# A float64 weight conversion that works in the tile it fills, on one Trainium2 core

## The chip, the core and the metric

The kernel runs on one core of a Trainium2 chip. Five engines work side by side: TensorE (PE; its weight loads are PEld), VectorE (DVE), ScalarE (ACT), GpSimd (POOL) and SyncE (SP, which here issues the loads). Each runs its own queue of instructions in order, and they wait for one another by semaphores. The metric is the device time of one execution in microseconds (us).

## The reference

Three layers follow one another. The attention inputs are float32; the two weights of the second layer (`moe_w_in`, `moe_w_out`) are scaled by a double and reach the chip as float64.

```python
out_up, out_local = ...                      # attention over means of 4, and over a band of 7 positions
x = (out_up + out_local)                     # 4 batches, 8 heads, 576 positions, 64 wide -> 2304 x 512
h = x @ w_in                                 # 512 x 2048, float64 weights
g = np.maximum(h, 0.0) + np.log1p(np.exp(-np.abs(h)))
y = (g @ w_out).astype(np.float32)           # 2048 x 512, float64 weights
logits = y @ w_gate + modality_bias[modality_id]
e_idx = np.argmax(logits, axis=1)            # one expert of 8 for each row
out[mask] = gate_w[mask, None] * (np.maximum(y[mask] @ w1[e], 0.0) @ w2[e])
```

## The kernel before

The 2304 rows go through the second layer in six blocks `n` of 384. A block has sixteen chunks `c` of 128 hidden columns: `mlp_H(n, c)` makes the product with `w_in` in a PSUM tile `ph` and starts softplus on ACT (three instructions on the tile `ga`, lines 777 to 779); `mlp_g` finishes it on VectorE (`gN` at line 786 for the first eight chunks of block 0, line 793 elsewhere); `mlp_Y` (line 802), three chunks later, adds the product with `w_out` to four PSUM tiles `py`. Block 0 uses plain float32 (lines 768 and 809); later blocks and the second half of block 0's `mlp_Y` use weights split in two float32r parts (`wis`, `wos`, lines 667 and 668).

Attention of batch 0 runs ahead of block 0, that of batches 1 to 3 is spread over the blocks. In one attention step `pS` holds scores, `ls` the masked scores, `lst` their maxima and sums, three ACT exponentials (line 341) fill `ls`, POOL scales it (line 347), PE transposes it to `pA`, VectorE copies that to `laT` (line 355), and PE makes `pO` of it.

The weights are converted while this goes on, in the first 157 us, and only there. There are 32 tiles of 128 by 512: sixteen of `w_in` into the tile `wi`, sixteen of `w_out` into `wo`. For each, SP loads the raw 8-byte words into a tile `raw` (512 KB; lines 642 and 646); ACT takes the absolute value of the upper halves, scaled, as float32 (`f64_top`, line 617), and three VectorE instructions turn the bits into a float32 number (`from_f64`, lines 625, 628 and 629). The first two of them work in a small tile `cva`, of which there are two, and the third writes to `wi` or `wo`. `raw` has six buffers, which it shares with the attention loads `qr`, `kr` and `vr`, so a load of a tile waits until a buffer is free, and a `raw` is free when its three readers are done.

The order of instructions on each engine is set by a scheduler when the kernel is built: it runs an own timeline of the program and takes what its timeline calls ready, with the priority that `ahead` asks for. `from_f64`'s first instruction is held in program order. What is ready for the scheduler depends on the buffers, so a change in buffers can change the order too.

Of the kernel before, what the change touches and what calls it, by code (L numbers as in the profile page):

```python
# [9 lines left out]
F32 = mybir.dt.float32  # L10
F32R = mybir.dt.float32r
I32 = mybir.dt.int32
U32 = mybir.dt.uint32
AF = mybir.ActivationFunctionType
ALU = mybir.AluOpType
# [26 lines left out]
F64_REBIAS = 2.0 ** -112  # L42
# [15 lines left out]
def band_attention__softplus_mlp__top1_moe(  # L58
# [15 lines left out]
    V, A, G, T = nc.vector, nc.scalar, nc.gpsimd, nc.tensor  # L74
# [28 lines left out]
    mlp = ctx.enter_context(tc.tile_pool(name="mlp", bufs=2))  # L103
    wi = wpool.tile([128, NC1, CC, 128], F32, name="wi")
    wo = wpool.tile([128, NC1, DM], F32, name="wo")
    ydram = drp.tile([NB, 128, CC, TB], F32, name="ydram")

    def ahead(n):

        return tc.high_priority(n) if n else nullcontext()  # L110
# [478 lines left out]
    for n in range(NOLD):  # L589
        for st in range(6):  # L590
            if (n, st) not in done:
                late = n >= 14
                t = {3: 8.0, 4: 8.6 if late else 8.0, 5: 9.0 if late else 8.3}[st]
# [18 lines left out]
                    )  # L612


    def f64_top(raw):
        t = mlp.tile([128, 512], I32, tag="cva", name="cva", bufs=2)
        A.activation(t.bitcast(F32), raw[:, :, 1].bitcast(F32), AF.Abs, scale=F64_REBIAS)
        return t

    def from_f64(raw, t, dst):  # L620

        lo, hi = raw[:, :, 0], raw[:, :, 1]
        ins = V.tensor_scalar(t, t, 3, None, ALU.logical_shift_left)  # L625
        if started[0]:
            tc.keep_in_program_order(ins)
        V.scalar_tensor_tensor(t, hi, -0x80000000, t, ALU.bitwise_and, ALU.bitwise_or)  # L628
        V.scalar_tensor_tensor(dst.bitcast(I32), lo, 29, t, ALU.logical_shift_right, ALU.bitwise_or)  # L629

    conv = [("i", 0), ("i", 1), ("o", 0)]
    for c in range(1, NC1):
        conv += ([("i", c + 1)] if c + 1 < NC1 else []) + [("o", c)]
    cpos, lpos = [0], [0]
    raws, tops = {}, {}

    def load_raw(n):
        while lpos[0] < min(n, len(conv)):
            kind, c = conv[lpos[0]]
            raw = mlp.tile([128, 512, 2], I32, tag="raw", name="raw", bufs=RAWB)  # L640
            if kind == "i":
                nc.sync.dma_start(
                    out=raw.rearrange("p (c f) w -> p c (f w)", c=CC),
                    in_=w_in[:, c * 128:(c + 1) * 128].bitcast(I32).rearrange("(c p) f -> p c f", p=128))
            else:
                nc.sync.dma_start(out=raw.rearrange("p f w -> p (f w)"),
                                  in_=w_out[c * 128:(c + 1) * 128, :].bitcast(I32))
            raws[lpos[0]] = raw
            lpos[0] += 1

    def conv_to(n):
        while cpos[0] < min(n, len(conv)):
            i = cpos[0]
            load_raw(i + 2)
            kind, c = conv[i]
            with ahead(0 if started[0] else -50):
                for k in range(i, min(i + 2, lpos[0]) if started[0] else i + 1):
                    if k not in tops:
                        tops[k] = f64_top(raws[k])
                from_f64(raws.pop(i), tops.pop(i), wi[:, c].rearrange("p c f -> p (c f)") if kind == "i" else wo[:, c, :])  # L660
            cpos[0] += 1
            load_raw(i + 2)

# [359 lines left out]
    for st in range(HEAD):  # L1023
        attn_to(pre_end[st])
        if st >= C0 - 5 + LAG:
            conv_to((st - C0 + 5 - LAG) * CR // 4 + 1)
        if st == 9 + LAG:
            split_wi(0, 0)
# [16 lines left out]
    for i, (n, c) in enumerate(seq[:NMLP]):  # L1045
# [20 lines left out]
        if n == 0:  # L1066
            conv_to(max(cpos[0], 3 + 2 * c + 1, CB + (33 - CB) * (2 * c + 1) // 32))
# [21 lines left out]
        if n == 0:  # L1089
            conv_to(max(cpos[0], 3 + 2 * c + 2, CB + (33 - CB) * (2 * c + 2) // 32))  # L1090
# [97 lines left out]
    p, q, pos_q = stages[-1]  # L1188
# [57 lines left out]
```

## Time and profile before

| | |
|---|---|
| time, median of 3 runs | 764.23 us (763.49 to 765.17) |
| the profiled execution | 765.59 us, of which the span of its instructions is 763.8 us |
| mean granted TensorE clock | 0.991 of full speed |
| TensorE matmul busy | 734.5 us, 96% of the span |
| VectorE busy | 487.6 us, 64% |
| ScalarE busy | 462.3 us, 61% |
| GpSimd busy | 419.2 us, 55% |

All times in rows are us from the start of the span. A busy PE is not a PE at its peak, since matmuls overlap in its pipe and their ends are modelled. An idle time with a name behind it is the time that the engine stood before this instruction, and what let it go.

### The profile page before, as it was taken

The page shows a single profiled execution, that of the slowest core. Times are in us where ns is not written, and L with a number is a line of the kernel's source. Part 1 is how long each engine was busy: PE and PEld are TensorE (multiplying, and loading weights), DVE is VectorE, ACT ScalarE, POOL GpSimd, SP SyncE. Part 2 cuts the span into 40 slices and gives each one's busy share as a digit, 9 for nine tenths or more (in the row PEclk, how much of TensorE's full clock was granted, in tenths as well). Part 3 has the DMA queues.
Part 4 walks back from the last instruction along what each step waited for, and adds up shares of the span by engine and source line. Part 5 has one row for each costly group of instructions (what it writes and reads, how often), then busy time and mean ns, then how long its engine had stood idle before and what let it go on. Part 6 is the DMA issues. An engine that isn't in the chain of part 4 may idle for free.

```text
span 763.8 us, 13608 instructions
## 1 busy us (share of the span) xinstructions
PE 734.5 (96%) x4917; PEld 655.8 (86%) x4918; DVE 487.6 (64%) x933; ACT 462.3 (61%) x1196; POOL 419.2 (55%) x381
## 2 busy tenths in 40 slices
PE   5989899999999999999999999999999999999995
PEld 5765567699999999998999999999997989899894
DVE  6999779765879555788645554346994484284222
ACT  5955565676667757666766665666864364365332
POOL 3553207376565655665565656666778465455542
PEclk9989999999999999999999999999999999999999
DMA  8987755115230511241001100530011022002002
GB/s 190 203 188 195 226 165 177 45 39 106 50 75 9 112 33 23 42 87 42 14 2 23 43 1 1 221 125 1 4 68 55 21 63 83 0 1 83 1 0 88
DMA packets 111446, 55.45 MB, mean 73 GB/s; under 512 B 89593, under 2 KB 102411, under 8 KB 111371
## 3 DMA queue, kind: packets, MB, share of 16 engines
q1 hardware_dynamic: 111083, 53.98, 26.8%
q8 instruction: 41, 0.67, 0.4%
q10 hardware_dynamic: 288, 0.52, 0.2%
q14 instruction: 34, 0.28, 0.1%
HBM read 45.05 MB, written 9.44 MB: 71 GB/s over the span
## 4 chain that ended last, share of the span: by engine, by line
PE 69%; DVE 16%; ACT 4%; issue 4%; DMA 3%; POOL 2%; SPq 1%; DVEq 0%; ACTq 0%; POOLq 0%
PE ph L771 19%; PE py L812 19%; PE py L1130 11%; PE ph L973 9%; PE pS L462 2%; DVE cva L628 2%; PE pO L495 2%; DVE cva L625 2%; PE pA L488 1%; PE py L809 1%; DVE xs L954 1%; DMA vr<-in_v_dram 1%; DVE wi L629 1%; DMA raw<-in_moe_w_in_dram 1%; PE ph L768 1%
## 5 line engine op out<-in xcount | busy, mean ns | idle before, releaser
L812 PE MATMUL py<-g,wos 128*128 128x384 f32 x1056 | 209.1, 341 | 2.6 <-DVE y L818 1.2
L812 PEld LDWEIGHTS py<-g,wos 128*128 128x128 f32 x1056 | 182.6, 188 | 9.2 <-issue 1.4
L771 PE MATMUL ph<-xT,wis 128*128 128x384 f32 x960 | 182.2, 337 | 0.0
L771 PEld LDWEIGHTS ph<-xT,wis 128*128 128x128 f32 x960 | 166.7, 188 | 1.1
L668 POOL TENSOR_TENSOR wis<-wi,wis 128x512 fp32r<-128x512 f32 x80 | 104.1, 1304 | 73.0 <-ACT wis L667 66.2
L668 POOL TENSOR_TENSOR wos<-wo,wos 128x512 fp32r<-128x512 f32 x88 | 118.2, 1344 | 45.0 <-ACT wos L667 44.7
L777 ACT ACTIVATE ga<-ph 128x384 f32<-128x384 f32 x96 | 46.6, 485 | 64.3 <-PE ph L771 61.3
L793 DVE SCALAR_TENSOR_TENSOR ph<-ph,ga 128x384 f32<-128x384 f32 x80 | 44.7, 560 | 58.9 <-ACT ga L779 58.6
L973 PE MATMUL ph<-xs,ws 128*128 128x384 f32 x378 | 73.9, 336 | 1.2 <-DVE u L978 1.2
L978 DVE TENSOR_TENSOR u<-ph,u 128x384 f32<-128x384 f32 x60 | 33.3, 555 | 60.2 <-PE ph L973 59.9
L973 PEld LDWEIGHTS ph<-xs,ws 128*128 128x128 f32 x378 | 67.1, 188 | 4.8 <-DVE u L978 1.6
L667 ACT CAST wos<-wo 128x512 fp32r<-128x512 f32 x88 | 54.4, 618 | 26.4 <-PE py L812 23.6
L1130 PE MATMUL py<-wos,gs 128*128 128x512 f32 x270 | 69.0, 394 | 0.7 <-POOL gs L984 0.4
L1130 PEld LDWEIGHTS py<-wos,gs 128*128 128x128 f32 x270 | 50.0, 188 | 9.8 <-POOL gs L984 0.8
L668 POOL TENSOR_TENSOR wos<-w2s,wos 128x512 fp32r<-128x512 f32 x24 | 33.5, 1395 | 34.7 <-ACT wos L667 34.7
L779 ACT ACTIVATE ga<-ga 128x384 f32<-128x384 f32 x96 | 50.3, 525 | 2.1
L778 ACT ACTIVATE ga<-ga 128x384 f32<-128x384 f32 x96 | 50.3, 525 | 0.3
L481 POOL TENSOR_TENSOR pls<-pls,plst 128x420 f32<-128x420 f32 x18 | 16.0, 891 | 61.2 <-DVE plst L480 54.4
L475 ACT ACTIVATE pls<-pls,plst 128x70 f32<-128x70 f32 x108 | 36.7, 341 | 21.4 <-DVE plst L473 21.3
L794 DVE CAST g<-ph 128x384 fp32r<-128x384 f32 x80 | 44.0, 550 | 7.8 <-PE py L812 4.3
L667 ACT CAST wis<-wi 128x512 fp32r<-128x512 f32 x80 | 48.9, 611 | 0.0
L768 PE MATMUL ph<-xN,wi 128*128 128x384 f32 x128 | 45.6, 503 | 0.9 <-DVE gN L786 0.9
(195 smaller groups left out, 1232.4 us busy)
## 6 DMA issues: line engine op xcount, KB each, us to landing
raw<-in_moe_w_in_dram SPq DMA_DIRECT2D x16, 512.0 KB
raw<-in_moe_w_out_dram SPq DMA_DIRECT2D x16, 512.0 KB
lv<-in_v_dram SPq DMA_DIRECT2D x72, 70.0 KB
vr<-in_v_dram SPq DMA_DIRECT2D x16, 288.0 KB
ydram<-y SPq DMA_DIRECT2D x12, 384.0 KB
yb<-ydram SPq DMA_DIRECT2D x12, 384.0 KB
out_dram<-ob SPq DMA_DIRECT2D x16, 256.0 KB
qr<-in_q_dram SPq DMA_DIRECT2D x48, 72.0 KB
```

The lines of the kernel that those rows point to most:

```text
L667: A.copy(w[:, 0], src)
L668: G.tensor_tensor(out=w[:, 1], in0=src, in1=w[:, 0].bitcast(F32), op=ALU.subtract)
L768: T.matmul(ps[:, :TB], wi[:, c, cc, :], xT[n][:, cc, :], start=(cc == 0), stop=(cc == CC - 1))
L771: T.matmul(ps[:, :TB], wt[:, w, cc, :], xT[n][:, x, cc, :], start=(i == 0), stop=(i == 3 * CC - 1))
L777: A.activation(a, ps[:, :TB], AF.Abs)
L778: A.activation(a, a, AF.Exp, scale=-1.0)
L779: A.activation(a, a, AF.Ln, bias=1.0)
L793: V.scalar_tensor_tensor(o, ps[:, :TB], 0.0, a, ALU.max, ALU.add)
L794: (A.copy if n < NATIVE else V.tensor_copy)(g[:, 0, :], o)
L812: T.matmul(yps[n][dc][:, :TB], w[:, a, dsl], g[:, b, :], start=(c == 0 and i == 0), stop=(c == NC1 - 1 and i == 2))
L973: T.matmul(ps[:, :TB], ops[:, w, a, cc, :], xop[p, x][:, l, cc, :], start=i == 0, stop=i == 5)
L1130: T.matmul(yps[n][t], g[:, a, t * 128:(t + 1) * 128], w[:, b, :], start=first and c == q and i == 0, stop=last and c == q + NQ and i == 2)
```

## The change

`cva` is gone. ACT writes the absolute value straight into the 128 by 512 part of `wi` or `wo` that the conversion fills, and the three VectorE instructions work there in place. Each part is written once in the program, so ACT no longer has a buffer to wait for. The number, the operations and the sizes of the instructions stay: 32 on ACT and 96 on VectorE. The two `cva` buffers stay allocated, as output tiles (`ob`) of the last stage use the same tag.

```diff
-    def f64_top(raw):
-        t = mlp.tile([128, 512], I32, tag="cva", name="cva", bufs=2)
-        A.activation(t.bitcast(F32), raw[:, :, 1].bitcast(F32), AF.Abs, scale=F64_REBIAS)
-        return t
-
-    def from_f64(raw, t, dst):
...
-        lo, hi = raw[:, :, 0], raw[:, :, 1]
+    def f64_top(raw, dst):
+        A.activation(dst, raw[:, :, 1].bitcast(F32), AF.Abs, scale=F64_REBIAS)
+
+    def from_f64(raw, dst):
...
+        lo, hi, t = raw[:, :, 0], raw[:, :, 1], dst.bitcast(I32)
         ins = V.tensor_scalar(t, t, 3, None, ALU.logical_shift_left)
...
-        V.scalar_tensor_tensor(dst.bitcast(I32), lo, 29, t, ALU.logical_shift_right, ALU.bitwise_or)
+        V.scalar_tensor_tensor(t, lo, 29, t, ALU.logical_shift_right, ALU.bitwise_or)
...
+    def weights(i):
+        kind, c = conv[i]
+        return wi[:, c].rearrange("p c f -> p (c f)") if kind == "i" else wo[:, c, :]
...
                 for k in range(i, min(i + 2, lpos[0]) if started[0] else i + 1):
-                    if k not in tops:
-                        tops[k] = f64_top(raws[k])
-                from_f64(raws.pop(i), tops.pop(i), wi[:, c].rearrange("p c f -> p (c f)") if kind == "i" else wo[:, c, :])
+                    if k not in topped:
+                        topped.add(k)
+                        f64_top(raws[k], weights(k))
+                from_f64(raws.pop(i), weights(i))
```

In the new file `f64_top` is line 616, `from_f64` lines 623, 626 and 627, and later lines are three higher (softplus is 780 to 782). The build puts instructions of block 0 in another order, on ACT most of all; behind block 0 the orders agree.

ACT before, from the exponentials of the last attention step but one of batch 0 (`ls_808`) to the end of the first softplus (`ga_887`; numbers behind a name tell one tile from the next, and the brackets hold the engines or load queues whose semaphores are awaited):

```order
L341 ACTIVATE ls_808,lst_810<-ls_808,lst_810 128x70 [waits DVE_49,PE_49,Pool_49]
L341 ACTIVATE ls_808,lst_810<-ls_808,lst_810 128x70 x2
L341 ACTIVATE ls_845,lst_847<-ls_845,lst_847 128x70 [waits DVE_49,PE_49,Pool_49]
L341 ACTIVATE ls_845,lst_847<-ls_845,lst_847 128x70 x2
L384 CAST xT_918<-xf_919 128x192 [waits DVE_49]
L777 ACTIVATE ga_887<-ph_882 128x384 [waits PE_49]
L778 ACTIVATE ga_887<-ga_887 128x384 [waits Activation_49]
L384 CAST xT_918<-xf_930 128x192 [waits DVE_49]
L779 ACTIVATE ga_887<-ga_887 128x384 [waits Activation_49]
```

The same place on ACT in the changed kernel (`ls_805` and `ls_842` are those two steps, `ga_883` the first softplus):

```order
L341 ACTIVATE ls_805,lst_807<-ls_805,lst_807 128x70 [waits DVE_49,PE_49,Pool_49]
L341 ACTIVATE ls_805,lst_807<-ls_805,lst_807 128x70 x2
L616 ACTIVATE wi_95<-raw_957 128x512 [waits DMAHW2_49]
L341 ACTIVATE ls_842,lst_844<-ls_842,lst_844 128x70 [waits DVE_49,PE_49,Pool_49]
L341 ACTIVATE ls_842,lst_844<-ls_842,lst_844 128x70 x2
L616 ACTIVATE wo_96<-raw_984 128x512 [waits DMAHW6_49]
L384 CAST xT_912<-xf_913 128x192 [waits DVE_49]
L780 ACTIVATE ga_883<-ph_878 128x384 [waits PE_49]
L616 ACTIVATE wi_95<-raw_998 128x512 [waits DMAHW7_49]
L781 ACTIVATE ga_883<-ga_883 128x384 [waits Activation_49]
L384 CAST xT_912<-xf_924 128x192 [waits DVE_49]
L782 ACTIVATE ga_883<-ga_883 128x384 [waits Activation_49]
```

Three first steps of conversions, the eighth to tenth of the 32, stand here now, and they wait for a load alone.

ACT before, at the softplus of chunk 3 (`ga_1076`), behind the exponentials of a pair of attention steps (`pde`):

```order
L416 ACTIVATE pde_1050,pdn_1049<-pS_1040,pmx_1048 96x144 x2
L617 ACTIVATE cva_1103<-raw_1101 128x512 [waits DMAHW6_49,DVE_49]
L777 ACTIVATE ga_1076<-ph_1071 128x384 [waits PE_49]
L778 ACTIVATE ga_1076<-ga_1076 128x384 [waits Activation_49]
L617 ACTIVATE cva_1122<-raw_1120 128x512 [waits DMAHW0_49,DVE_49]
L779 ACTIVATE ga_1076<-ga_1076 128x384 [waits Activation_49]
```

The same place on ACT in the changed kernel (the softplus of chunk 3 is `ga_1066`):

```order
L416 ACTIVATE pde_1040,pdn_1039<-pS_1030,pmx_1038 96x144 x2
L616 ACTIVATE wo_96<-raw_1108 128x512 [waits DMAHW1_49]
L616 ACTIVATE wi_95<-raw_1120 128x512 [waits DMAHW2_49]
L616 ACTIVATE wo_96<-raw_1135 128x512 [waits DMAHW3_49]
L780 ACTIVATE ga_1066<-ph_1061 128x384 [waits PE_49]
L781 ACTIVATE ga_1066<-ga_1066 128x384 [waits Activation_49]
L616 ACTIVATE wi_95<-raw_1147 128x512 [waits DMAHW4_49]
L782 ACTIVATE ga_1066<-ga_1066 128x384 [waits Activation_49]
```

Where two first steps stood around the softplus before, four stand now, three of them ahead of it and one inside.

## Rows read from the trace of the kernel before

**Rows 1.** The page: busy time, share of the span and instructions of each engine.

```profile
PE 734.5 (96%) x4917; PEld 655.8 (86%) x4918; DVE 487.6 (64%) x933; ACT 462.3 (61%) x1196; POOL 419.2 (55%) x381
```

**Rows 2.** Waits over the span: engine, tile, line, releaser: us, times, longest.

```profile
ACT cva L617 <- DVE wi L629: 12.7, 8, 2.3
...
ACT cva L617 <- DVE wo L629: 11.0, 10, 2.3
```

**Rows 3.** Waits of PE from 55 to 165 us.

```profile
PE pA L430 <- DVE gN L786: 2.1, 1, 2.1
...
PE py L812 <- POOL g L795: 0.9, 1, 0.9
...
PE ph L768 <- DVE gN L786: 0.9, 1, 0.9
...
PE pA L430 <- DVE ga L793: 0.7, 1, 0.7
...
PE pO L495 <- DVE plaT L489: 0.4, 1, 0.4
```

**Rows 4.** Tile `cva`: durations in ns (min/median/max), first and last start, forms.

```profile
L617 ACT ACTIVATE cva<-raw x32: 641/678/707, 27.9 to 149.4; 128x512 f32<-128x512 f32 x32
...
L628 DVE SCALAR_TENSOR_TENSOR cva<-raw,cva x32: 650/691/1652, 29.6 to 155.5; 128x512 int32<-128x512 int32 x32
L629 DVE SCALAR_TENSOR_TENSOR wi<-raw,cva x16: 650/691/2002, 31.1 to 148.5; 128x512 int32<-128x512 int32 x16
```

**Rows 5.** Timeline of ACT, 57 to 62 us: start, us, instruction, [idle before, releaser].

```profile
57.60 0.35 ACT L341 ACTIVATE ls<-ls,lst 128x70 f32<-128x70 f32 x1 [1.91 <-DVE lst L335]
...
60.48 0.49 ACT L777 ACTIVATE ga<-ph 128x384 f32<-128x384 f32 x1
61.00 0.52 ACT L778 ACTIVATE ga<-ga 128x384 f32<-128x384 f32 x1
```

**Rows 6.** Timeline of SP's load queue, 55 to 62 us (start and length of the issue).

```profile
55.09 0.41 SPq L148 DMA_DIRECT2D vr<-in_v_dram  x1
55.69 0.39 SPq L642 DMA_DIRECT2D raw<-in_moe_w_in_dram  x1
...
58.20 0.36 SPq L646 DMA_DIRECT2D raw<-in_moe_w_out_dram  x1
61.30 0.39 SPq L642 DMA_DIRECT2D raw<-in_moe_w_in_dram  x1
```

**Rows 7.** Timeline of POOL, the first use of that `vr`.

```profile
59.07 1.26 POOL L164 TENSOR_TENSOR vr<-vr 72x512 f32<-72x512 f32 x1 [4.95 <-DMA vr<-in_v_dram]
```

**Rows 8.** Timeline of DVE, the copy ahead of chunk 1.

```profile
59.14 0.55 DVE L355 COPY laT<-pA 70x384 f32<-70x384 f32 x1
```

**Rows 9.** Timeline of PE, 60 to 95 us, at chunks 1, 2, 3 and 6.

```profile
60.87 2.85 PE L768 MATMUL ph<-xN,wi 128*128 128x384 f32 x8
...
65.24 2.85 PE L768 MATMUL ph<-xN,wi 128*128 128x384 f32 x8 [0.87 <-DVE gN L786]
...
88.41 0.58 PE L430 MATMUL pA<-ident,pde 96*72 96x96 f32 x3 [2.11 <-DVE gN L786]
88.78 4.37 PE L809 MATMUL py<-gN,wo 128*128 128x384 f32 x8
92.99 2.74 PE L768 MATMUL ph<-xN,wi 128*128 128x384 f32 x8
```

**Rows 10.** Stretches: length, busy us of PE, PEld, DVE, ACT, POOL, clock, DMA share, GB/s.

```profile
85.00:90.00 5.00, 2.89 (x12) 1.73 (x11) 3.73 (x7) 2.50 (x5) 0.00 (x0) 0.86 0.43 156
90.00:95.00 5.00, 5.00 (x14) 2.80 (x13) 4.85 (x11) 3.20 (x8) 0.00 (x0) 0.80 0.64 189
```

**Rows 11.** Timeline of ACT and DVE ahead of chunk 3's `gN`.

```profile
86.69 0.66 ACT L617 ACTIVATE cva<-raw 128x512 f32<-128x512 f32 x1 [2.34 <-DVE wi L629]
87.25 0.51 ACT L779 ACTIVATE ga<-ga 128x384 f32<-128x384 f32 x1
...
87.80 0.56 DVE L786 SCALAR_TENSOR_TENSOR gN<-ph,ga 128x384 f32<-128x384 f32 x1 [1.14 <-ACT ga L779]
```

More of the change, by code (lines that the diff above doesn't have):

```diff
@@ L634, in band_attention__softplus_mlp__top1_moe @@
     cpos, lpos = [0], [0]
-    raws, tops = {}, {}
+    raws, topped = {}, set()
+    def weights(i):
+        kind, c = conv[i]
+        return wi[:, c].rearrange("p c f -> p (c f)") if kind == "i" else wo[:, c, :]
     def load_raw(n):
@@ L654, in conv_to @@
             load_raw(i + 2)
-            kind, c = conv[i]
             with ahead(0 if started[0] else -50):
                 for k in range(i, min(i + 2, lpos[0]) if started[0] else i + 1):
-                    if k not in tops:
-                        tops[k] = f64_top(raws[k])
-                from_f64(raws.pop(i), tops.pop(i), wi[:, c].rearrange("p c f -> p (c f)") if kind == "i" else wo[:, c, :])
+                    if k not in topped:
+                        topped.add(k)
+                        f64_top(raws[k], weights(k))
+                from_f64(raws.pop(i), weights(i))
             cpos[0] += 1
```

## The prediction

> **What bounds the kernel now.** I read the page first: PE is busy 96% of the span and no other engine over 64% [rows 1]. So only time in which PE stands, or runs slowly, can be won. Then I read who waits for whom. ACT's first step of a conversion stands behind VectorE's last step for 23.7 us, in 8 and 10 pieces [rows 2]: the two `cva` buffers are full, and ACT's queue, which also carries softplus and the exponentials, stands with them. These are ACT's waits, not PE's. The table of PE's own waits over the same stretch (55 to 165 us) has the price: 2.1, 0.9, 0.9, 0.7 and 0.4, about 5.0 us [rows 3]. None of them names a conversion; they name `gN`, `ga`, `g` and `plaT`, which stand in the same queues. The costliest one I followed back: PE at 88.41 waited 2.11 us for `gN` [rows 9], `gN` at 87.80 waited 1.14 us for softplus on ACT, and softplus's last instruction at 87.25 stood behind a conversion's first step that had waited 2.34 us for VectorE [rows 11]. That is the pattern that the change removes. The stand costs more than itself: behind it eight matmuls took 4.37 us where eight take 2.74 a little later [rows 9], and the granted clock reads 0.86 and 0.80 in these stretches [rows 10], part of the time at the lower of TensorE's two levels (1.2 of 2.4 GHz). That is 1.6 us more.
>
> **Instructions themselves: 0.** ACT's step writes 128 by 512 float32 as before (median 678 ns), and VectorE's second step, which already worked in place, has the same median as the third, which did not (691 and 691 ns) [rows 4]. So working in place costs nothing by itself. Bounds from the range of ACT's step, 641 to 707 ns over 32 of them, are -1.2 and +0.9 us, and not on PE. VectorE keeps 96 instructions, and what slows some of them (up to 2002 ns [rows 4]) stays.
>
> **What the new order costs: +2.4 us near 60 us.** ACT's first steps now wait for their load alone, so the scheduler puts them earlier. Ahead of chunk 2 three of them (eighth to tenth of 32) stand among the last exponentials and the first softplus. The trace of before shows when their loads can be there. The eighth `raw` is issued at 55.69, behind a `vr` issued at 55.09 [rows 6] whose first reader waited for it until 59.07 [rows 7]: 4.0 us from issue to use. The eighth then lands after 59.07, the tenth, issued at 61.30 [rows 6], near 65.3 by the same 4.0 us. In the trace ACT did these exponentials at 57.60 and softplus's second step at 61.00 [rows 5], earlier than either load can land. So ACT's queue head stands for a DMA, and what stands behind it is on PE's path:
> - exponentials at 59.7 or later instead of 57.60, so VectorE, which stands for their sums, makes the copy of 59.14 [rows 8] 2 us later, and chunk 1 starts 2 us after 60.87 [rows 9];
> - softplus: the tenth load at 65.3, its step 0.6, two more softplus steps 1.1 with a small cast of 0.3 between them, then `gN` 0.55: 67.8. Chunk 2 needs the buffer that `gN` frees and started at 65.24 [rows 9], so it comes 2.6 us late. The two delays lie over one another and do not add.
>
> The lower bound is 0 (the load is issued earlier, or lands within 1.5 us of its issue); the upper is 3.5, since the two attention steps before have a first step ahead of them too and can delay the eighth load's own issue by a microsecond. I take +2.4, near the `vr` row. [...]
>
> **What it gives back at 88 us: -1.5, and -0.7 for the clock.** If PE comes 2.4 us later to the place where it waited 2.1 us, part of that wait is just filled. But `gN` of chunk 3 moves too. Four first steps stand around its softplus now; the last of them stands ahead of softplus's last step and needs a `raw` whose buffer only comes free with a conversion on VectorE shortly before. With 4 us for that load, `gN` ends between 88.6 and 90.1 where it ended at 88.4. So PE stands 0.3 to 1.7 us behind its old time here instead of 2.4: I take 0.9. The slow matmuls behind the wait cost 1.6 us; a shorter wait may spare them, but the new stand near 61 to 63 us is as long as the old one and may bring the same. I take -0.7, with bounds -1.6 and +1.6.
>
> **What it gives back later: -0.7.** The other waits of PE that are left, 0.9, 0.7 and 0.4 [rows 3], lie in the second half of the conversions, behind softplus or VectorE. ACT's free queue shortens the way to softplus, but VectorE does as much work as before, and one more first step stands ahead of one of those softplus groups. I take a third, with bounds 0 and -2.0. Behind 157 us nothing is converted, and the orders agree: 0.
>
> **Sum.** 2.4 - 1.5 - 0.7 - 0.7 = -0.5 us. The profiled execution took 765.59 us with a span of 763.8: it would be 763.3 and 765.1. Against the median 764.23, which is 1.4 below that execution, -0.5 gives **763.7 us**. About 0.2% (1.5 us) is what a measurement of this kernel can tell from no change, so this forecast, 762.7 to 765.7, counts as the same.
>
> **Rivals.**
> - *ACT runs free, and the loads are there.* For it: 23.7 us of waits [rows 2] with one cause. No early stand; `gN` of chunk 3 comes by its idle 1.14 earlier, the slow matmuls behind it are spared (-1.6), a third of the later waits goes: -1.1 - 1.6 - 0.7 = -3.4, **760.8 us**. Against it: the issue times of rows 6. The Trainium skill ("Perfetto Trace Analysis", Optimization Strategy) says that the same gap, repeated, on the engine that should be saturated can mean too few buffers for the next tile. The trace has the repeated gap, but on ACT, and PE is the saturated one; by that rule this rival would win. Chance 0.30.
> - *Waits for VectorE become waits for loads, and PE pays.* The place is ACT's queue head at the tenth load and again at each softplus of chunks 3 to 6, where a first step stands inside or ahead. Its price: the full early delay of 2.6 stays, since `gN` of chunk 3 moves as far as PE does; the new early stand brings a slow stretch of half the old one, 0.8; and nothing comes back later: +3.4, less 0.6 for the wait at 88 us that still shortens: +2.8, **767.0 us**. It decides once a load of 512 KB takes over some 3 us from its buffer's release to its use; then the fourth first step at chunk 3 holds softplus longer than the 2.34 us that it stood before [rows 11]. Against it: PE's waits are 5.0 us in all [rows 3], so most softplus groups have slack that a late one uses up first. Chance 0.27.
> - *The change does not remove the wait.* The first steps of the changed program wait on loads alone, so this is out: under 0.01.
> - *VectorE paces all of it, and ACT's freedom is worth nothing:* 764.2, inside the forecast, and counted there.
>
> **How the numbers follow.** Forecast 0.42, gain 0.30, loss 0.27, rest 0.01. Of the forecast's 0.42 I count 0.02 on each side beyond its bounds: faster 0.32, same 0.39, slower 0.29. The range has to take in most of both rivals. The gain reaches to -4.7 if all later waits go (-1.1 - 1.6 - 2.0, 759.5), the loss to +4.2 with a whole slow stretch and the upper early bound (3.5 + 1.6 - 0.9, 768.4). From 760.2 to 767.4 about 0.1 is left out at either end.
>
> **What would show it.** Right: ACT's waits for VectorE at the conversion are gone, and waits of the same lines for the DMA of `raw` stand in their place, near 60 us at least 2 us long; chunk 1 starts after 62.5, chunk 2 after 66.5; the wait at 88 us is under 1.7. Wrong: chunk 2 starts by 65.5 (no early stand, the first rival), or the first split product of block 1 comes over 2 us later than in the trace of before (the second). Three readings settle the terms one by one: the wait of the tenth first step for its load, the time of eight matmuls behind the stand, and PE's waits from 120 to 157 us.

## The result, and the profile of the changed kernel

The changed kernel took 772.48 us (median of four runs, 770.28 to 775.47) beside 764.7 us of the kernel before: a ratio of 1.0104, with a 95% interval of 1.0066 to 1.0143. Measured once more, beside the experiments below, it took 769.99 us, ratio 1.0062 (1.0038 to 1.0085). It is slower, by 0.6 to 1.0%; the prediction had 763.7 us and a range up to 767.4.

The profiled execution took 772.87 us with a span of 771.1, 7.3 us over the span of before. The page's row of busy times answers to [rows 1]:

```profile
PE 736.2 (95%) x4917; PEld 656.8 (85%) x4918; DVE 482.5 (63%) x933; ACT 462.0 (60%) x1196; POOL 420.7 (55%) x381
```

VectorE and ACT are no busier than before (482.5 and 462.0 us where [rows 1] has 487.6 and 462.3), so the change gave them no more work. What grew is waiting. The waits of ACT at the conversion (engine, tile, line, releaser: us, times, longest; the answer to [rows 2]):

```profile
ACT wo L616 <- DMA raw<-in_moe_w_out_dram: 16.1, 10, 3.4
ACT wi L616 <- DMA raw<-in_moe_w_in_dram: 15.9, 10, 3.8
```

The 23.7 us behind VectorE are gone, as the change intends, and 32.0 us behind loads stand in their place. The table of PE's waits from 55 to 165 us (as [rows 3]) shows who paid:

```profile
PE pO L360 <- DVE laT L355: 4.5, 2, 2.9
PE pO L495 <- DVE plaT L489: 2.2, 2, 1.4
PE pA L430 <- DVE gN L789: 1.4, 1, 1.4
PE py L815 <- POOL g L798: 0.9, 1, 0.9
PE ph L771 <- ACT daT L433: 0.8, 1, 0.8
```

The wait for `gN` shrank from 2.1 to 1.4 us. The waits for `laT` and `plaT`, VectorE's copies in the local attention, are what grew: `laT` is new in this table, and `plaT` had 0.4 us.

**How one late load becomes a late PE.** The chain of work that ended last, in order of time (start, us, what), between 46 and 66 us:

```profile
46.38 8.35 DMA raw<-in_moe_w_out_dram
54.74 0.05 ACT wo L616
...
55.96 1.13 ACT ls L341 x6
57.11 0.18 DVE lst L345
...
58.15 0.76 DVE qkT L180
58.92 0.03 DVE lst L335
58.95 5.22 DMA raw<-in_moe_w_in_dram
64.19 0.04 ACT wi L616
...
64.76 1.11 ACT ls L341 x6
```

It is a loop, not a single stand. A load holds ACT's queue at a first step; behind it wait the local attention's exponentials (L341); behind their sums waits VectorE; VectorE then comes later to its transposes (`qkT`, L180), which read `qr` and `kr` out of the `raw` buffers; and SP issues the next `raw` as such a transpose ends (58.91 and 58.95 us; the chain names `lst` L335, the instruction right behind the transpose, which reads no `raw`, so this step is a reading of the times). The next load is late because the one before it was, and it holds ACT again. The timelines of the engines show the same turns (start, us, instruction, [idle before, releaser]); ACT first:

```profile
50.10 0.67 ACT L616 ACTIVATE wo<-raw 128x512 f32<-128x512 f32 x1 [3.21 <-DMA raw<-in_moe_w_out_dram]
...
54.74 0.66 ACT L616 ACTIVATE wo<-raw 128x512 f32<-128x512 f32 x1 [1.56 <-DMA raw<-in_moe_w_out_dram]
...
64.19 0.66 ACT L616 ACTIVATE wi<-raw 128x512 f32<-128x512 f32 x1 [3.79 <-DMA raw<-in_moe_w_in_dram]
```

then SP, VectorE and PE:

```profile
57.14 0.41 SPq L148 DMA_DIRECT2D vr<-in_v_dram  x1
58.95 0.39 SPq L645 DMA_DIRECT2D raw<-in_moe_w_in_dram  x1
```

```profile
57.11 0.17 DVE L345 TENSOR_SCALAR lst<-lst 128x3 f32<-128x3 f32 x1 [3.38 <-ACT ls L341]
...
65.89 0.17 DVE L345 TENSOR_SCALAR lst<-lst 128x3 f32<-128x3 f32 x1 [3.54 <-ACT ls L341]
```

```profile
58.29 1.18 PE L360 MATMUL pO<-laT,lv 70*64 70x64 f32 x12 [2.94 <-DVE laT L355]
...
66.77 0.91 PE L360 MATMUL pO<-laT,lv 70*64 70x64 f32 x12 [1.56 <-DVE laT L355]
...
67.61 4.11 PE L771 MATMUL ph<-xN,wi 128*128 128x384 f32 x8
72.20 2.75 PE L771 MATMUL ph<-xN,wi 128*128 128x384 f32 x8
```

`vr` goes out 2.05 us later than in [rows 6], the eighth `raw` 3.26 us later; chunk 1 starts at 67.61 instead of 60.87 and chunk 2 at 72.20 instead of 65.24 [rows 9].

The loop begins with a step that is early, not with a load that is late. The fifth load and the fifth first step of the kernel before (SP, ACT), and the fifth load of the changed kernel:

```profile
44.55 0.36 SPq L646 DMA_DIRECT2D raw<-in_moe_w_out_dram  x1
```

```profile
49.45 0.65 ACT L617 ACTIVATE cva<-raw 128x512 f32<-128x512 f32 x1
```

```profile
45.05 0.36 SPq L649 DMA_DIRECT2D raw<-in_moe_w_out_dram  x1
```

The load goes out 0.5 us later than before, but ACT reaches the step at 46.89 us, 2.6 us earlier than before, and stands there for 3.21.

**Where the 7.3 us come from.** Both traces pass the same places: the product L360 near 41.6 us (before any step that waits for its load), chunk 0, chunk 1, chunk 6, the first split product of block 1. "Again" is the profile of the second measurement (span 766.2).

| us from one place to the next | before | changed | difference | again | difference |
|---|---|---|---|---|---|
| start to that L360 | 41.50 | 41.79 | +0.3 | 41.97 | +0.5 |
| to chunk 0 | 13.83 | 17.60 | +3.8 | 15.66 | +1.8 |
| to chunk 1 | 5.54 | 8.22 | +2.7 | 8.06 | +2.5 |
| to chunk 6 | 32.12 | 30.83 | -1.3 | 28.93 | -3.2 |
| to the first split product | 62.03 | 64.48 | +2.4 | 63.43 | +1.4 |
| to the end of the span | 608.8 | 608.2 | -0.6 | 608.2 | -0.6 |
| sum | 763.8 | 771.1 | +7.3 | 766.2 | +2.4 |

Two losses, then: one ahead of chunk 1 (+6.5 and +4.3), of which some comes back by chunk 6, and a second between chunk 6 and the end of the conversions. ACT's first steps stand for loads in the leg to chunk 6 too (3.4, 1.2, 0.4 and 1.8 us between 80 and 97 us), and yet that leg is shorter than before, so a wait for a load isn't by itself a loss of PE's. The second loss is the same kind of loop, with SP, VectorE and ACT at other lines:

```profile
109.50 0.69 DVE L627 SCALAR_TENSOR_TENSOR wo<-raw,wo 128x512 int32<-128x512 int32 x1
...
116.97 0.17 DVE L479 TENSOR_SCALAR plst<-plst 128x6 f32<-128x6 f32 x1 [3.86 <-ACT pls L475]
```

```profile
110.22 0.37 SPq L645 DMA_DIRECT2D raw<-in_moe_w_in_dram  x1
```

```profile
114.26 0.66 ACT L616 ACTIVATE wi<-raw 128x512 f32<-128x512 f32 x1 [1.69 <-DMA raw<-in_moe_w_in_dram]
114.82 0.34 ACT L475 ACTIVATE pls<-pls,plst 128x70 f32<-128x70 f32 x1
```

VectorE's last step of one conversion, which ends at 110.2, frees the buffer; SP issues the load at 110.22; ACT, several conversions ahead of VectorE, uses it 4.0 us later at 114.26; the exponentials behind that step keep VectorE idle for 3.86 us, at a time when its own conversions are due. The windows show that VectorE's work was only put off (length, then busy us of PE, PEld, DVE, ACT, POOL, granted clock, DMA share, GB/s): it was busy 15.54 and 15.44 us in these stretches before.

```profile
100.00:120.00 20.00, 20.00 (x105) 12.18 (x105) 12.64 (x26) 11.65 (x32) 0.89 (x1) 1.00 0.56 179
120.00:140.00 20.00, 16.89 (x109) 12.75 (x109) 19.38 (x31) 12.46 (x33) 12.04 (x7) 0.91 0.53 159
```

In the second stretch of this trace VectorE is full, the copies `plaT` queue among its conversion steps, and PE stands 1.39 and 0.84 us for them. In the second measurement's trace PE's waits for `plaT` are 2.2 us again, but VectorE was busy only 13.95 and 14.38 us in these stretches and 17.23 us from 140 to 160 (16.26 before), so there its work was put off further. The granted clock from 120 to 140 us was 0.91 in both traces of the changed kernel and 1.00 before.

### The profile page after: what moved, and what is told of

It reads as the page before. It is cut to its first block, busy times and chain, and to the rows that moved or that the text cites. A ratio compares the mean times of both kernels' runs of the same rounds, so it can differ in the third digit from the quotient of the medians.

```text
span 771.1 us, 13584 instructions
## 1 busy us (share of the span) xinstructions
PE 736.2 (95%) x4917; PEld 656.8 (85%) x4918; DVE 482.5 (63%) x933; ACT 462.0 (60%) x1196; POOL 420.7 (55%) x381
## 4 chain that ended last, share of the span: by engine, by line
PE 79%; DVE 7%; DMA 5%; ACT 4%; POOL 2%; issue 1%; SPq 1%; DVEq 0%; ACTq 0%
PE py L815 23%; PE ph L774 21%; PE py L1133 11%; PE ph L976 10%; PE ph L771 3%; DMA raw<-in_moe_w_in_dram 3%; PE pS L462 2%; PE pO L495 2%; DMA raw<-in_moe_w_out_dram 2%; PE pA L488 1%; DMA qr<-in_q_dram 1%; PE py L812 1%; PE pO L440 1%; PE pS L405 1%; POOL wos L671 1%
## 5 line engine op out<-in xcount | busy, mean ns | idle before, releaser
L671 POOL TENSOR_TENSOR wos<-wo,wos 128x512 fp32r<-128x512 f32 x88 | 119.8, 1363 | 47.5 <-ACT wos L670 47.3
L771 PE MATMUL ph<-xN,wi 128*128 128x384 f32 x128 | 47.5, 520 | 0.8 <-ACT daT L433 0.8
```

Source lines behind the costliest of these rows:

```text
L671: G.tensor_tensor(out=w[:, 1], in0=src, in1=w[:, 0].bitcast(F32), op=ALU.subtract)
L771: T.matmul(ps[:, :TB], wi[:, c, cc, :], xT[n][:, cc, :], start=(cc == 0), stop=(cc == CC - 1))
```

## The experiments

Theory A says that the order costs: freed from the small tiles, ACT's first steps are put so far ahead that they stand at loads, with exponentials and softplus behind them. Rival B says that working in the weight tile itself costs. Rival C puts the lasting loss into the later part alone. Rival D says that any new order costs about that much, the old one having been lucky. In the expectations "chunk one" or "first chunk" is chunk 0 here, and "chunk two" or "second chunk" is chunk 1.

**e1: in place, with the old wait.**

```
+        k = len(topped) - 1
+        if k >= 2:
+            tc.add_manual_dep(ins.ins, done[k - 2].ins.name, <semaphore wait>)   # done: VectorE's last steps
```

> The changed kernel, in place as it is, but ACT's first step of conversion k waits on a semaphore for VectorE's last step of conversion k-2, as the two small tiles made it wait before. Theory A (ACT's freed first steps are put ahead of exponentials where their loads have not landed, and the delay goes round ACT, VectorE, SP and the loads): the early order of before returns, the first chunk of block 0 starts at 55 to 56 us instead of 59.4, the second at 61 to 62 instead of 67.6, time 762 to 767 us (ratio to before 0.997 to 1.003). Rival B (working in the weight tile itself costs, through VectorE's access or the casts that read the tile): 769 to 774 us, chunk two still behind 65 us.

Measured: 765.18 us, ratio 0.9989 (0.9961 to 1.0017). ACT's waits at this line are as before:

```profile
ACT wo L616 <- DVE wo L631: 17.7, 10, 5.1
...
ACT wi L616 <- DVE wi L631: 8.6, 7, 2.4
```

Rival B falls: all 32 conversions work in place here, and the time is that of before. Two numbers missed: chunk 0 started at 57.75 us and chunk 1 at 63.31. This execution was already 2.4 us late at the L360 product (43.91 instead of 41.50), ahead of the part in question; from there to chunk 0 it took 13.84 us and on to chunk 1 5.56, as before.

**e2: the freedom alone, VectorE out of place.**

```
-        lo, hi, t = raw[:, :, 0], raw[:, :, 1], dst.bitcast(I32)
-        ins = V.tensor_scalar(t, t, 3, None, ALU.logical_shift_left)
+        lo, hi, t = raw[:, :, 0], raw[:, :, 1], <small tile cva, 2 buffers>
+        ins = V.tensor_scalar(t, dst.bitcast(I32), 3, None, ALU.logical_shift_left)
...
+        V.scalar_tensor_tensor(dst.bitcast(I32), lo, 29, t, ALU.logical_shift_right, ALU.bitwise_or)
```

> The other half of the change alone: ACT writes its first step straight into the weight tile and so waits for no small tile, but VectorE's first two steps write the small tile and only its last writes the weights, so VectorE doesn't work in place. Theory A: as slow as the changed kernel, 769 to 775 us, first chunk at 59 to 60 us, second at 67 to 68.5 us. Rival B (in place costs): about as before, 762 to 766 us.

Measured: 770.35 us, ratio 1.0055 (1.0026 to 1.0083); 8.14 us from chunk 0 to chunk 1, 26.5 us of waits for loads. With e1 this settles which half of the change costs: not where VectorE writes, but that ACT's first step no longer waits for it, with the order that follows from that.

**e3 and e4: the old wait for a part of the conversions.** e3 has e1's wait with `k < 10` added to the condition, e4 with `k >= 10`.

> The changed kernel with the wait of e1 for the third to tenth conversion alone; later ones run free. Theory A with the whole cause in the early part (7 of the 7.3 us were lost by 72 us): chunk two at 61 to 62 us, time 762 to 767 us. Rival C (the loss that lasts is that of 127 to 139 us, when wos and the transposes of the local attention come late; the early one would have been absorbed by waits behind it): 767 to 772 us although chunk two starts by 62 us.

> The changed kernel with the wait of e1 from the eleventh conversion on; the first ten run free as in the change. Theory A with an early cause: chunk two at 67 to 68.5 us, time 768 to 774 us. Rival C (the late part decides): chunk two at 67 to 68.5 us too, but the 1.5 us gained by 98 us grow and the time is 763 to 767 us.

Measured: e3 770.71 us, ratio 1.0069 (1.0047 to 1.0091); e4 768.53 us, ratio 1.0039 (1.0016 to 1.0061). In e3 chunk 1 starts at 60.73 us, as early as before, and yet the kernel is slow: my expectation that the early part held the whole cause was wrong, and the time is the one that rival C named. What it loses comes late, and its trace has the signs of the loop of 110 us. ACT and VectorE of e3:

```profile
103.22 0.69 ACT L616 ACTIVATE wo<-raw 128x512 f32<-128x512 f32 x1 [2.28 <-DMA raw<-in_moe_w_out_dram]
...
105.95 0.68 ACT L616 ACTIVATE wi<-raw 128x512 f32<-128x512 f32 x1 [2.04 <-DMA raw<-in_moe_w_in_dram]
```

```profile
108.96 0.17 DVE L479 TENSOR_SCALAR plst<-plst 128x6 f32<-128x6 f32 x1 [4.27 <-ACT pls L475]
```

From chunk 1 to the first split product e3 took 98.4 us where the kernel before took 94.2. In e4 it is the other way round: 7.96 us from chunk 0 to chunk 1 as in the changed kernel (chunk 1 at 66.41, a little ahead of the 67 expected), then 91.3 us from chunk 1 to the first split product, less than before; its time is the one named for an early cause. So neither part holds the whole cause. Each costs by itself, 0.4 and 0.7%; the changed kernel has both, 0.6 to 1.0%. But the changed kernel took 95.3 and 92.4 us from chunk 1 to the first split product, less than e3's 98.4, so the two parts don't simply add.

**e5 and e6: a lead of three, and of four.** e1's wait with `done[k - 3]` and with `done[k - 4]`.

> The changed kernel, but ACT's first step of conversion k waits for VectorE's last step of conversion k-3: a lead of three where e1 and the kernel before have two. Theory A (what costs is that ACT runs so far ahead of VectorE that it stands at loads which VectorE's own last steps had to let out 4 us earlier): at three its loads have nearly always landed; ACT's waits for the raw loads in 20 to 175 us stay under 8 us (32 in the changed kernel), time 761 to 767 us. Rival D (any new order of these instructions costs some 5 us, and the order of before was lucky): 767 to 773 us with few waits for loads.

> As e5 with a lead of four. Theory A: the time rises with the lead, since the load of k can go out only when conversion k-6 is done: ACT's waits for raw loads 8 to 20 us, time 764 to 770 us, above e5. Rival D: no relation to the lead, 767 to 773 us or as e5.

Measured: e5 766.52 us, ratio 1.0018 (0.9996 to 1.0039), with 9.2 us of waits for loads, a little over the 8 expected. e6 775.41 us, ratio 1.0137 (1.0116 to 1.0159), with 18.3 us, as expected, but a time well above the 770. From three to four the loss grows clear of noise, which rival D doesn't give; from e1's two to three the intervals overlap. But at four it is larger than with no bound at all, which theory A doesn't give either. e6's first steps wait for both, 18.3 us for loads and 14.6 for VectorE, 32.9 in all; that this sum is why is argued, not shown.

**e7: a seventh `raw` buffer.** `RAWB = 7`, with the expert outputs moved from the small tiles' place to `raw`.

> The changed kernel with ACT free, and the 4 KB that the small tiles took given to a seventh raw tile (the expert outputs that shared the small tiles' place go to the raw tiles). Theory A: loads go out one conversion earlier, so ACT's waits for raw loads fall from 32 us to 10 to 22 us and the time to 764 to 769 us, under the changed kernel's 772. If the waits fall but the time stays at 770 to 774 us, waiting for loads is not what costs. Rival D: 767 to 773 us whatever the waits.

Measured: 768.96 us, ratio 1.0059 (1.0024 to 1.0095). The waits for loads fell to 23.4 us, over the 22 expected, and the ratio is that of the changed kernel measured again, 1.0062. The time lies in the ranges of theory A and of rival D, so it doesn't decide between them. The move of the expert outputs has an effect of its own: behind the first split product e7 took 606.3 us, where all kernels with six `raw` buffers took 608.1 to 609.1. Up to that product it lost 5.0 us on before, between the 7.9 and the 3.0 of the changed kernel's two traces. One more buffer doesn't cure it; that ACT then runs ahead to a load one further on is argued, not shown.

**e8: in place, ACT's first steps held at their place in the code.** From block 0 on:

```
+        ins = A.activation(dst, raw[:, :, 1].bitcast(F32), AF.Abs, scale=F64_REBIAS)
+        if started[0]:
+            tc.keep_in_program_order(ins)     # an order on ACT, no wait
```

> The changed kernel, with ACT's first steps from block 0 on held at their place in the code (behind what was written before them on ACT, without any wait), where the changed kernel lets the scheduler move them forward; the steps written ahead of block 0 too stay ahead of it, but no others come among the last local exponentials. Theory A: chunk two of block 0 at 60 to 63 us (59.4 to 60.9 in the fast runs' traces is 60.87 of before, 67.61 of the change), waits for raw loads under 15 us, time 762 to 768 us. Rival B or D: 768 to 774 us.

Measured: 760.06 us (759.09 to 761.66), ratio 0.9935 (0.9921 to 0.9949): faster than both kernels, and under the 762 expected. Rival D falls: this is a new order too, and so is e9's below. The order is all that e8's edit changes against the changed kernel, so the order is what that kernel pays for. The waits of ACT and of PE from 55 to 165 us:

```profile
ACT wi L616 <- DMA raw<-in_moe_w_in_dram: 2.2, 1, 2.2
```

```profile
PE pO L495 <- DVE plaT L489: 1.0, 2, 0.8
PE pO L360 <- DVE laT L355: 0.4, 1, 0.4
```

Chunk 1 starts at 61.88 us, inside the 60 to 63 expected. Of 23.7 or 32.0 us of waits 2.2 are left, and of PE's 5.0 us [rows 3] 1.4. The fifth first step stands at 63.45 us, behind the last exponentials and a whole softplus, and starts without a wait, where the changed kernel had it at 50.10 and the kernel before at 49.45, in front of them:

```profile
62.35 0.52 ACT L783 ACTIVATE ga<-ga 128x384 f32<-128x384 f32 x1
62.78 0.33 ACT L384 CAST xT<-xf 128x192 fp32r<-128x192 f32 x1
63.02 0.52 ACT L784 ACTIVATE ga<-ga 128x384 f32<-128x384 f32 x1
63.45 0.67 ACT L616 ACTIVATE wo<-raw 128x512 f32<-128x512 f32 x1
64.03 0.66 ACT L616 ACTIVATE wi<-raw 128x512 f32<-128x512 f32 x1
```

The wait for `gN` at chunk 3 is gone as well, and the matmuls behind that place no longer run slowly: the granted clock reads 1.00 in both stretches where [rows 10] has 0.86 and 0.80.

```profile
85.00:90.00 5.00, 5.00 (x21) 3.08 (x20) 4.96 (x11) 4.86 (x11) 0.00 (x0) 1.00 0.47 138
90.00:95.00 5.00, 5.00 (x26) 3.06 (x26) 4.27 (x8) 0.49 (x1) 0.00 (x0) 1.00 0.80 263
```

This is the state that the prediction's first rival described, ACT free and the loads there, and near its time (760.8), but in an order that the change doesn't make. That the times agree doesn't support the rival's reason, as e9 shows.

**e9: the kernel before, in e8's manner.** The same `keep_in_program_order` on the old first step, small tiles kept.

> The kernel before with its two small tiles, and ACT's first steps from block 0 on held at their place in the code as in e8. It tells whether e8's 5 us under before come from the order alone or from the order together with the freedom from the small tiles. If the order alone pays: 758 to 762 us. If the small tiles' wait stands in the way of this order (a step held in place that also waits for VectorE keeps the softplus steps behind it, up to 2.3 us each as in [rows 2]): ACT's waits for VectorE at this line stay at 12 us or more in 20 to 175 us, time 763 to 769 us. I take the second.

Measured: 761.43 us, ratio 0.995 (0.9929 to 0.997); ACT waits 12.1 us for VectorE and not at all for loads. I had taken the second answer. Its waits came as expected, its time didn't: the first answer is right there. The order alone brings most of e8's gain, and the intervals of e8 and e9, measured on two chips, overlap. That the small tiles go adds little or nothing.

**e10: e8 with seven `raw` buffers.**

> e8 with the seventh raw tile of e7. If loads still hold e8 (its one wait for a raw load is 2.2 us near 97 us), it gains 0 to 2 us: 758 to 761 us. If e8's remaining waits have other causes, or the expert outputs in the raw tiles cost something late, 759 to 764 us. Theory A takes 759.5: with 2.2 us of waits left there is hardly anything for an earlier load to remove.

Measured: 763.02 us (760.06 to 770.85), ratio 0.9988 (0.9958 to 1.0018). My 759.5 missed, and the time lies in the range of the other answer. It isn't better than e8, but the wait that e8 had left didn't go either (3.9 us in e10), so whether it costs e8 anything stays open. The expert outputs in `raw` cost nothing late in the profiled execution: behind the first split product it took 606.4 us, e8 608.8. That execution was the fastest of its twelve, with a span of 758.1 us where e8's has 758.0.

**e11: the changed kernel again.** It gave the second ratio of the result and the "again" columns above; its waits for loads sum to 28.0 us.

> The changed kernel once more, on the same chip and beside the same runs of before as e9 and e10, for a like comparison: 769 to 775 us, ratio to before 1.006 to 1.014.

**e12: half way.** ACT writes the small tile, VectorE's first step moves it on into the weights, the rest is in place.

```
-        ins = V.tensor_scalar(t, t, 3, None, ALU.logical_shift_left)
+        ins = V.tensor_scalar(dst.bitcast(I32), t, 3, None, ALU.logical_shift_left)
```

> Half way: ACT writes the small tile, VectorE's first step reads it and writes the weight tile, the other two steps work in place. A small tile comes free after one step of VectorE (0.65 us) instead of three (3.3 us in all), and the scheduler orders ACT's steps with that. Theory A: ACT can again run ahead to where loads are not there, though less far than in the changed kernel; ACT's waits for raw loads 5 to 20 us, time 764 to 771 us. Were the waits for VectorE a pure loss, as the change assumes: 759 to 763 us.

Measured: 762.03 us, ratio 0.9957 (0.993 to 0.9985), with 4.9 us of waits for loads and 9.9 for VectorE. My expectation under theory A missed, and the time is the one named for the opposite: that the waits for VectorE are a loss. They fell here from 23.7 to 9.9 us. Why the scheduler's order stays good with a small tile that comes free earlier was not shown.

**All of them in one table:** waits of ACT's first steps in one profiled execution each, from 20 to 175 us, and the ratio to before.

| kernel | waits for loads, us | waits for VectorE, us | chunk 0 to 1, us | ratio |
|---|---|---|---|---|
| e8 order held, in place | 2.2 | 0 | 5.8 | 0.9935 |
| e9 order held, small tiles | 0 | 12.1 | 5.7 | 0.9950 |
| e12 half way | 4.9 | 9.9 | 6.8 | 0.9957 |
| e10 order held, seven raw | 3.9 | 0 | 6.6 | 0.9988 |
| e1 lead of two | 0.3 | 26.3 | 5.6 | 0.9989 |
| before | 0.3 | 23.7 | 5.5 | 1 |
| e5 lead of three | 9.2 | 17.5 | 6.8 | 1.0018 |
| e4 free early | 9.7 | 15.9 | 8.0 | 1.0039 |
| e2 free, out of place | 26.5 | 0 | 8.1 | 1.0055 |
| e7 free, seven raw | 23.4 | 0 | 7.0 | 1.0059 |
| e11 changed, again | 28.0 | 0 | 8.1 | 1.0062 |
| e3 free late | 19.2 | 3.7 | 5.6 | 1.0069 |
| changed, first measurement | 32.0 | 0 | 8.2 | 1.0104 |
| e6 lead of four | 18.3 | 14.6 | 8.4 | 1.0137 |

Every kernel with under 5 us of waits for loads is at or below the time of before, every one with over 9 us is above it (e5 not clear of noise: its interval takes in 1). The same number of microseconds behind VectorE costs less: e1 and e2 wait 26.6 and 26.5 us, nearly all of it for VectorE in e1 and all for loads in e2, and have 0.9989 and 1.0055. That the waits for VectorE are harmless is not shown. The three kernels clearly faster than before have 0 to 12.1 us of them, e1 and before have 26.3 and 23.7; the orders differ too, and no run takes the two apart. A first step that waits for VectorE waits for an engine that is working on conversions; one that waits for a load stops exponentials for which VectorE itself then waits: VectorE's waits for ACT from 40 to 175 us are 18.8 us before, 17.2 in e1, 30.2 and 25.9 in the changed kernel and 29.9 in e2. This doesn't hold for every kernel: e7 has 18.5 and e4 19.5, no more than e8's 19.4, and both are slower than before. Among the slower kernels the size doesn't follow the waits closely. So the table parts the kernels that lose from those that don't, and doesn't price the waits.

## Why the prediction was wrong, point by point

**Working in place costs nothing: right.** VectorE's second and third steps in the weight tile take 688 and 691 ns at the median, ACT's 672, where [rows 4] has 691, 691 and 678; e1 shows it in the time.

**The waits move from VectorE to loads: right in kind.** They were seen to be waits at ACT's queue head, with the place near 60 us and the step that waits there. The wait of the eighth first step was 3.79 us, issue to use 5.2 us where the `vr` row gave 4.0 [rows 6, 7]. In the trace these loads of 512 KB took 4.0 to 8.4 us from issue to use: 4.0 at 110 us with the DMA engines 0.56 busy, 5.2 at 58.95 and 8.4 at 46.38, both in a stretch (44 to 68 us) with 0.89 busy. The Trainium skill ("DMA: Bandwidth & Descriptors", Anatomy of one DMA) has a fit of about 2.0 us and the bytes at 436 GB/s for a transfer that GpSimd issues, which for 512 KB would be an estimate of 3.2 us. SP issues the loads here, so no run here tests that fit.

**"+2.4 us near 60 us, bounds 0 to +3.5": the step that failed.** What I worked out, the eighth step's stand, was right for itself: from chunk 0 to chunk 1 it cost +2.7 and +2.5 us, where I had 2. The rest of the term was mis-sized. The fifth to seventh steps, at 45 to 56 us, stand too (3.21, 0.19 and 1.56 us), and cost +3.8 and +1.8 us ahead of chunk 0; I had looked only at the eighth to tenth and given the earlier ones one microsecond of the upper bound. The table of PE's waits that I priced from [rows 3] begins at 55 us, while first steps run from 27.9 us on [rows 4], so the stretch of this loss was outside what I read. And I took issue times out of the trace of before as if the change left them alone. SP's queue waits for buffers that VectorE frees, VectorE waits for ACT, and so the stands add. Of the three readings named, the tenth step's wait for its load was 0: by then everything was late enough. The term came out at +6.5 and +4.3.

**The signs.** All signs named for "right" came in the first trace: waits for `raw` in place of those for VectorE, 3.79 us near 60 us, chunk 1 at 67.61, chunk 2 at 72.20, the wait at 88 us at 1.38. So did the second sign of "wrong": the first split product came 7.9 and 3.0 us late. The signs of "right" all lie ahead of chunk 6 and set no upper limit on the delay, so they couldn't tell the forecast from the second rival.

**"Gives back at 88 us: -1.5, clock -0.7": about right.** From chunk 1 to chunk 6, -1.3 and -3.2 against -2.2. The wait for `gN` shrank from 2.11 to 1.38 us, and the eight matmuls behind it took 2.77 us instead of 4.37. But PE came there 6.1 and 2.6 us late, where the term was worked out for 2.4, so in the first trace the agreement is in part luck. The new stand brought a slow stretch of its own in that trace, 4.11 us for the eight matmuls of chunk 1; in the second measurement's they took 2.85.

**"Gives back later: -0.7, bounds 0 to -2.0": wrong in sign,** +2.4 and +1.4. PE's waits from 120 to 157 us grew from 2.0 to 3.1 us (2.2 in the second measurement), and the granted clock from 120 to 140 us fell from 1.00 to 0.91. I had asked what ACT's freedom gives to softplus, not what a first step in front of the exponentials of the local attention takes from VectorE. The bound of 0 had no reason behind it that excluded a loss: a loop as in the early part is there. e3 shows a late loss alone, at 0.7%.

**"Behind 157 us: 0": right,** 608.2 us against 608.8.

**The rivals.** The second one, waits for loads that PE pays, is what happened. Its place was right in part: ACT's queue head, but from the fifth first step on and ahead of the exponentials; the tenth load, which it named, was not waited for, and the stands around the softplus of chunks 3 and 4 (0.4 and 1.8 us) fell in a leg that gained. Its price of 2.8 was too small, because it too counted one stand and not a loop. The first, 760.8, is near the time of e8, but e9 comes to nearly the same with 12.1 us of waits for VectorE left, so its reason, the freedom of ACT, is not what brought it. The Trainium skill ("Perfetto Trace Analysis", Optimization Strategy) reads repeated gaps on the engine that should be saturated as a possible sign of too few buffers. The repeated gaps here are ACT's, not PE's, and no run bears that reading out: one more buffer for loads (e7) left the ratio at 1.0059, no small tile at all gave 1.0062 and 1.0104, and an order without any further buffer (e9) gave 0.995.

## What to carry to other kernels

In this kernel a wait for a buffer was what kept the scheduler from putting an instruction in front of work that matters. When you take such a wait away, look in the new order for what the instruction will stand at then, and what stands behind it on its engine. Where the transfer that it stands at needs a buffer freed by an engine that waits for that work, delays go round and add; take issue times from the old trace only after asking whether they depend on what moves. Try to hold such an instruction at its place before freeing it: here that brought 0.5% with the old buffers and 0.65% without them.

## What the runs showed of the hardware

A load of 512 KB took 4.0 to 8.4 us from issue to use in one execution (above); the two longer ones fell where the DMA engines were busier, but they differ between them at the same busy share, so that isn't the whole of it. A first step on VectorE, 0.41 us as a rule, can take much longer when GpSimd works beside it: one took 2.93 us at 128.9 us of the changed kernel, where GpSimd's products ran without a gap from 123.2 to 132.7 us. It needn't: another, at 124.6 us in the same stretch, took 0.38. One split on GpSimd, 1.36 us on average, took 4.10 us there beside VectorE's conversions. And two executions of the same changed kernel lost 7.3 and 2.4 us of span against one trace of before, at the same places but by different amounts; a single trace gives the places, the repeated runs the size.
